# The second gate one expert earlier, and low parts of weights on VectorE while it is worked out

## The chip, the cores and the metric

One core of one Trainium2 chip. The metric is device time in microseconds of one execution; the kernel before has a median of 983.49 us in 3 runs (981.95 to 984.66). TensorE multiplies matrices; VectorE, ScalarE and GpSimd work on tiles in SBUF (GpSimd also issues the indirect DMAs); SyncE (SP) issues the other DMAs. Each engine takes its instructions in the order in which the kernel writes them.

## The reference

Causal block attention (4 batches, 8 heads, 576 positions of 64), then two layers of experts over 2304 tokens of width 512. In the first, each token goes to its best two of eight experts, in the second to one. Cut to the routing and one expert:

```
noisy = x @ w_gate + log1p(exp(x @ w_noise)) * noise
top2  = two largest of noisy, weighted by their softmax
for e in range(8):                      # first layer, 512 -> 1024 -> 512
    out[mask] += top2_w * (relu(x[mask] @ w1[e]) @ w2[e])
logits = out @ w_gate2 + modality_bias[modality_id]
e_idx  = argmax(logits)                 # second layer: one expert each
out2[mask] = softmax(logits)[e_idx] * (relu(out[mask] @ m2w1[e]) @ m2w2[e])
```

## The kernel before

Each matrix is split into a high part, which TensorE takes in a fast format (`wh`, `xth`, `hh`), and a low part, the rest (`wl`, `xtl`, `hl`); a product is three matmuls. ScalarE casts the high part; the low part is a subtraction. For weights that subtraction (`Stage.split`, 128 x 1024) is on the engine that the caller hands in.

The work after attention is a list of jobs that `run` (line 1418) goes through. A job is one expert (or part of one) over a group of tokens: its first half, `mm1`, makes eight blocks of the hidden layer; its second, `mm2`, makes one tile of 128 tokens at a time in PSUM (three such tiles, `py`). During `mm1`, `run` splits this job's second weights and gathers the next job's token rows (`rows`, an indirect DMA on GpSimd); during `mm2` it transposes the rows that have been gathered (`cols`: TensorE into the one tile `px`, ScalarE `xth`, VectorE `xtl`) and splits the next job's first weights (`between`).

Order of the jobs: parts of experts 0 and 1, the rest of 0, experts 2 to 7 (five token tiles each; E is 8, so E-3, E-2 and E-1 are experts 5, 6 and 7), and then the second layer's six groups (`seconds`): groups 1 and 2 of 512 tokens from the first table (k = 0), groups 3 and 4 of 512 and two of 256 from the second (k = 1). The expert of a group is known only at run time and is read into a register on SP.

When a tile of a first-layer expert is done, its rows are added to `X2` in DRAM by an indirect DMA, and eight dot products on VectorE (`zero<-py,gts,wide`, reading the result in PSUM) give what it adds to the second gate's logits; a further indirect DMA adds them to `LG`, with a 1 that counts how many of its two experts a token has behind it. After the last such add of a job, its `then` is called.

`gates(k)` (line 1478) is a generator of some eighty small steps, nearly all on VectorE. It loads `LG` (`lgx`), takes the tokens that are complete (k = 0) or complete and not yet placed (k = 1), counts them by expert (small matmuls into `pt`), fixes which expert each group gets (`eg0`, `eg1`, `egs`) and writes lists of slots (`ids00`, `ids10`, `ids11`: `sl_ob`, `sl_oa`, `sl_ov`, matmuls into `pt`, then `si_*`). `starts` gives counts and first groups per expert, `experts_of` the expert of each group. For k = 1 it also makes `more` and `eo`, which only a loop at the very end of the kernel reads.

The order of instructions on every engine is written out by a planner: `clk` adds up a modelled cost of each instruction, `walk` runs a generator's steps at modelled times, `filler` puts waiting dot products in whenever VectorE's modelled clock is at most 0.4 us (0.2 while the flag `chain` is set, that is while `gates` runs) ahead of TensorE's, and `room` forces out the oldest ones when more than two tiles of them wait. A job's gathers are issued once the flag of its slots is set.

Of the kernel before, what the change touches and what calls it, by code (L numbers as in the profile page):

```python
# [30 lines left out]
def moe_kernel(tc, q, k, v, w_gate, w_noise, noise, w1, w2, mod_id, w_gate2, mod_bias, m2w1, m2w2, out):  # L31
# [25 lines left out]
    def bc(ap, shape):  # L57
        return ap.to_broadcast(shape)
# [47 lines left out]
    with ExitStack() as top:  # L106
# [362 lines left out]
        class Job:  # L469
# [21 lines left out]
            def gather(s, t):  # L491
                xr = rp.tile([128, DM], F32, name="xr", bufs=5)
                i = gps.indirect_dma_start(out=xr, out_offset=None, in_=s.table,
                                                 in_offset=bass.IndirectOffsetOnAxis(ap=s.ic(t), axis=0))
                if s.apart is not None:
                    for o in s.apart:
                        tc.declare_no_dep(i.ins, o.ins, reason="rows of other tokens")
                    early_rows.append(i)
                s.xr.append(xr)
                if s is j11:  # L500
                    s.due.append(max(clk["dve"], clk["pool"]) + 2.5)
# [96 lines left out]
        last_rows, early_rows = [], []  # L598

        def add_rows(ids, c0, nt, then=None):  # L600
            last = c0 + nt == NA1
            prev = last_rows if last else []
            placed_ = []

            def f(t, yr, py, g):
                c = c0 + t
                i = gps.indirect_dma_start(out=X2, out_offset=bass.IndirectOffsetOnAxis(ap=ids[:, c:c + 1], axis=0),
                                                 in_=yr, in_offset=None, compute_op=OP.add)
                for o in prev + (early_rows if last else []):
                    tc.declare_no_dep(i.ins, o.ins, reason="rows of other tokens")  # L610
                prev.append(i)
                note(yr, py, g, ids[:, c:c + 1], placed_, then if t == nt - 1 else None)
            return f

        def job1(e, t0=0, nt=NP, then=None, need=(None, None)):
            return Job((w1[e], w2[e]), X1, nt, lambda t: ids1[:, e * NP + t0 + t:e * NP + t0 + t + 1],
                       lambda t: gts1[:, e * NP + t0 + t:e * NP + t0 + t + 1], add_rows(ids1, e * NP + t0, nt, then), need, 128 if nt == 2 else UNIT)
# [35 lines left out]
        j11.wa, j11.wb = j10.wa, j10.wb  # L653
        chain = lambda k, p: lambda: walk(gates(k), now[0] + .5, p)
        firsts = [job1(0, FIRST[0], NP - FIRST[0], need=(None, "ids1"))]
        firsts += [job1(e, then={E - 2: chain(0, 1), E - 1: chain(1, 1)}.get(e), need=(None, "ids1")) for e in range(2, E)]
        seconds = [job2(k, g) for k in range(2) for g in range(NW)] + [job2(1, g, True) for g in range(NSM)]
        stage = Stage([j00, j10] + firsts + seconds)

# [758 lines left out]
        def run(jobs, hp_, ea, eb, nxt=None, stage=stage):  # L1418

            ah = 4  # L1420
            fs = (0, 1, 3, 5)
            for n, j in enumerate(jobs):
                nx = jobs[n + 1] if n + 1 < len(jobs) else nxt

                def rows():
                    if nx and nx.ready(1) and len(nx.xr) < nx.nt:
                        nx.gather(len(nx.xr))

                eb_ = [gps, gps, vec, vec] if j is firsts[0] else eb
                for f in range(len(j.hh), NF // 128):  # L1430
                    j.mm1(f, hp_)
                    if f in fs and len(j.wb) < NQ:
                        stage.split(eb_[fs.index(f) % len(eb_)] if "ids1" in flags else vec)
                    stage.fetch(ah)
                    rows()
                    filler()
                    tick(j.n * .005)
                left = [0, 0, 2 * j.nt]

                def between():  # L1440
                    left[2] -= 1
                    if nx:
                        if left[2] == 0 and not nx.ready(1):
                            until(nx.need[1])
                        while left[2] < 2 and nx.ready(1) and len(nx.xr) < nx.nt:
                            nx.gather(len(nx.xr))
                        while left[0] < len(nx.xr) and (left[2] == 0 or left[0] < 2 * j.nt - left[2]):
                            if left[2] and left[0] < len(nx.due) and nx.due[left[0]] > clk["pe"]:
                                break
                            nx.cols(left[0])  # L1450
                            left[0] += 1
                            if nx is j10 and left[0] == nx.nt:
                                at(clk["pe"] + .5, spread)
                            if left[2] >= nx.nt - left[0]:
                                break
                        while len(nx.wa) < NQ and left[1] < NQ * (2 * j.nt - left[2]) / (2 * j.nt):
                            if not stage.ring and not nx.ready():
                                if left[2]:
                                    break
                                until(nx.need[0])  # L1460
                            stage.split(ea[left[1] % len(ea)] if "ids1" in flags else vec)
                            left[1] += 1
                    stage.fetch(ah)
                    filler()
                    tick(2.56)

                for t in range(j.nt):
                    j.mm2(t, between)
                    rows()
                    between()  # L1470
# [7 lines left out]
        def gates(k):  # L1478
# [37 lines left out]
            if k == 1:  # L1516
                nr = pool.tile([128, E], F32, name="g_nr")
                vec.scalar_tensor_tensor(nr, gn, -float(GW), pp[:, NTT], op0=OP.mult, op1=OP.add)
                yield .3
                gm, gr = yield from starts(pool, nr, th2, "q_")  # L1520
                yield from experts_of(pool, gm, gr, egs, "q_")
                flags.add("egs")
                vec.tensor_scalar(gr, gr, 2.0, float(BW * NW), op0=OP.mult, op1=OP.add)
                yield .3
                vec.scalar_tensor_tensor(gr, gn, -float(BW), gr, op0=OP.mult, op1=OP.add)
                yield .3
                vec.tensor_add(nr, gs, gn)
                yield .3
                vec.tensor_scalar(nr, nr, NW + .5, 1e5, op0=OP.is_gt, op1=OP.mult)
                yield .3  # L1530
                vec.tensor_add(gs, gs, nr)
                yield .3
                go, s_ = yield from starts(pool, base, th1, "o_")
                vec.tensor_copy(gso, s_)
                yield .3
                yield from experts_of(pool, go, gso, eo, "o_")
            t0, pos, st = tl("t0", sh), tl("pos"), tl("st")
            vec.tensor_tensor(t0, pp[:, 0:NTT], oh, op=OP.mult)
            yield .3
# [14 lines left out]
                vec.scalar_tensor_tensor(w, s2, float(GW), pos, op0=OP.mult, op1=OP.is_gt)  # L1554
                yield .3
            if k == 1:
                vec.tensor_tensor(t0, oh, bc(gr[:, None, :], sh), op=OP.mult)
                yield .3
                vec.tensor_reduce(s2, t0, axis=AX, op=OP.add)
                yield .3  # L1560
                vec.scalar_tensor_tensor(st, st, float(BW), s2, op0=OP.mult, op1=OP.subtract)
                yield .3
                vec.tensor_tensor(st, st, w, op=OP.mult)
                yield .3
                vec.tensor_add(st, st, s2)
                yield .3
# [7 lines left out]
            if k < 2:  # L1574
                new = tl("new") if k else placed
                vec.tensor_scalar(new, a, cap - .5, None, op0=OP.is_lt)
                yield .3
                if k:
                    vec.tensor_add(placed, placed, new)
                    yield .3  # L1580
                    held = tl("held", dt=BF16)
                    vec.tensor_copy(held, placed)
                    yield "pe", 0
                    pm = ps_r.tile([128, NTT], F32, name="pt")
                    ten.matmul(pm, ones, held, start=True, stop=True)
                    yield .4
                    m = pool.tile([1, 1], F32, name="g_m")
                    vec.tensor_reduce(m, pm[0:1], axis=AX, op=OP.add)
                    yield .3
                    vec.tensor_scalar(more, m, float(NT) - .5, None, op0=OP.is_lt)  # L1590
                    yield .3

            vec.tensor_tensor(l, l, bc(mx[:, :, None], sh), op=OP.subtract)
# [11 lines left out]
            for i0_, a0 in enumerate(range(0, cap, 2 * HG)):  # L1605
# [9 lines left out]
                yield .3  # L1615
                yield from slot_ids(pool, acc, na, NTT, pad2[:, a0:a0 + na], ids[:, a0:a0 + na], gts[:, a0:a0 + na])
                flags.add("ids%d%d" % (k, i0_ > 0))
            flags.discard("chain")

        with sp():  # L1620
# [131 lines left out]
```

## Time and profile before

| | |
|---|---|
| median of 3 runs | 983.49 us |
| profiled execution | 984.59 us, its span 982.8 us, mean granted clock 0.989 |
| VectorE busy | 681.4 us (69%) |
| ScalarE busy | 482.6 us (49%) |
| GpSimd busy | 489.6 us (50%) |
| HBM | 126 GB/s over the span |

Busy is the sum of the times in which an engine ran something; the idle time of an engine that sets no end costs nothing. Stages follow each other in time: attention until about 300 us, the first layer until 738, the second to the end.

### The profile page before, as it was taken

To read this page: it belongs to the slowest core of one execution; us is meant where nothing else is said; L and a number is where in the kernel's file an instruction comes from. 1 tells how busy PE (TensorE), PEld (TensorE's weight loads), DVE (VectorE), ACT (ScalarE), POOL (GpSimd) and SP (SyncE) were. 2 spreads that over 40 slices of the span, in tenths; PEclk is the share of its full clock that TensorE was granted. 3 is DMA by queue.
4 is the path that set the end of the run, shared out by engine and by line. 5 is a ranking of instruction groups with operands and counts; after the bars stand their busy time and mean duration, and the time that the engine had idled before them with its cause. 6 is when DMAs were issued, how large, how long until landed. Compare 5 with 4: busy or idle time off the path is not lost.

```text
span 982.8 us, 16351 instructions
## 1 busy us (share of the span) xinstructions
PE 943.6 (96%) x5661; PEld 835.6 (85%) x5661; DVE 681.4 (69%) x1676; ACT 482.6 (49%) x1090; POOL 489.6 (50%) x472
## 2 busy tenths in 40 slices
PE   9999998999999999999999999999889988999995
PEld 6989897998978999989898998989767876888894
DVE  6878779888889979395775939577877764433241
ACT  6989997987651344333333333433223332433352
POOL 6234343464325599585875848557374124222122
PEclk9999999999999999999999999999999999999998
DMA  6586742322196366374654627443554525443440
GB/s 128 104 216 192 233 122 70 78 60 68 58 337 156 68 187 165 111 158 97 130 128 116 122 76 171 99 76 47 161 113 124 181 79 175 137 130 108 138 130 13
DMA packets 145293, 124.49 MB, mean 127 GB/s; under 512 B 75626, under 2 KB 115946, under 8 KB 145075
## 3 DMA queue, kind: packets, MB, share of 16 engines
q1 hardware_dynamic: 126242, 90.14, 32.0%
q0 software_dynamic: 17904, 32.96, 16.7%
q8 instruction: 47, 0.77, 0.3%
q10 hardware_dynamic: 1056, 0.26, 0.1%
q14 instruction: 44, 0.35, 0.1%
HBM read 95.50 MB, written 28.09 MB: 126 GB/s over the span
## 4 chain that ended last, share of the span: by engine, by line
PE 70%; issue 11%; DVE 6%; POOL 5%; ACT 4%; DMA 3%; SPq 0%; POOLq 0%; ACTq 0%; DVEq 0%
PE py L73 25%; PE ph L73 25%; PE pt L73 8%; PE ps L73 6%; PE pa L73 3%; POOL wl L73 2%; PE px L73 2%; ACT p L73 2%; DMA raw<-in_moe_w_dram 1%; DVE wl L73 1%; DMA xr<-X,ids 1%; DVE PTl L73 1%; ACT kp L73 1%; DMA qld<-in_q_dram 1%; POOL out_dram L73 1%
## 5 line engine op out<-in xcount | busy, mean ns | idle before, releaser
L73 POOL TENSOR_TENSOR wl<-raw,wh 128x1024 fp32r<-128x1024 f32 x70 | 180.9, 2602 | 113.8 <-ACT wh L73 111.2
L73 DVE SCALAR_TENSOR_TENSOR zero<-py,gts,wide 128x512 f32<-128x512 f32 x304 | 227.6, 749 | 8.4
L73 PE MATMUL ph<-xth,wh 128*128 128x312 f32 (+4 forms) x672 | 217.2, 323 | 2.1 <-DVE kp L73 1.2
L73 PE MATMUL ph<-xtl,wh 128*128 128x312 f32 (+4 forms) x672 | 216.9, 323 | 0.2 <-DVE xtl L73 0.2
L73 PE MATMUL ph<-xth,wl 128*128 128x312 f32 (+4 forms) x672 | 217.1, 323 | 0.0
L73 PE MATMUL py<-wh,kp 128*128 128x512 f32 x488 | 166.0, 400 | 0.0
L73 PEld LDWEIGHTS ph<-xth,wh 128*128 128x128 f32 x672 | 127.4, 190 | 8.5 <-DVE kp L73 1.9
L73 PEld LDWEIGHTS ph<-xtl,wh 128*128 128x128 f32 x672 | 127.3, 189 | 6.0 <-DVE xtl L73 0.5
L73 PEld LDWEIGHTS ph<-xth,wl 128*128 128x128 f32 x672 | 126.9, 189 | 5.2
L73 ACT ACTIVATE yr<-py,gts 128x512 f32<-128x512 f32 x59 | 40.6, 688 | 165.0 <-PE py L73 109.3
L73 ACT ACTIVATE wh<-raw 128x1024 fp32r<-128x1024 f32 x112 | 117.8, 1052 | 2.1 <-DMA raw<-in_moe_w_dram 2.1
L73 PEld LDWEIGHTS py<-wh,kp 128*128 128x128 f32 x488 | 92.4, 189 | 19.0
L73 DVE SCALAR_TENSOR_TENSOR hl<-ph,hh 128x312 fp32r<-128x312 f32 (+5 forms) x84 | 43.0, 514 | 78.8 <-ACT hh L73 78.7
L73 PE MATMUL ps<-kh,kp 128*128 128x256 f32 (+5 forms) x320 | 95.9, 340 | 0.5 <-ACT p L73 0.3
L73 PE MATMUL py<-wl,kp 128*128 128x512 f32 x244 | 96.0, 394 | 0.0
L73 PE MATMUL py<-wh,hh 128*128 128x512 f32 x228 | 94.3, 413 | 0.0
L73 POOL DMA_INDIRECT xr<-X,ids x54 | 56.1, 1040 | 76.2 <-PE px L73 43.3
L73 PE MATMUL py<-wh,hl 128*128 128x512 f32 x228 | 90.9, 399 | 0.0
L73 PE MATMUL py<-wl,hh 128*128 128x512 f32 x228 | 90.5, 397 | 0.0
L73 ACT ACTIVATE hh<-ph 128x312 fp32r<-128x312 f32 (+5 forms) x84 | 38.4, 457 | 99.8 <-PE ph L73 99.6
L73 DVE TENSOR_TENSOR xtl<-px,xth 128x512 fp32r<-128x512 f32 (+1 forms) x57 | 38.9, 682 | 64.6 <-ACT xth L73 64.6
L73 ACT ACTIVATE kp<-ph 128x312 fp32r<-128x312 f32 (+5 forms) x84 | 38.4, 457 | 91.8 <-PE ph L73 91.4
(274 smaller groups left out, 1843.0 us busy)
## 6 DMA issues: line engine op xcount, KB each, us to landing
raw<-in_moe_w_dram SPq DMA_DIRECT2D x112, 512.0 KB, 3.6
X<-zero SPq DMA_DIRECT2D x13, 512.0 KB, 4.0
kld<-in_k_dram SPq DMA_DIRECT2D x32, 128.0 KB, 2.9
vld<-in_v_dram SPq DMA_DIRECT2D x32, 128.0 KB, 2.8
X<-x SPq DMA_DIRECT2D x16, 256.0 KB, 2.7
qld<-in_q_dram SPq DMA_DIRECT2D x30, 128.0 KB, 3.0
wide<-in_moe_w_dram SPq DMA_DIRECT2D x4, 512.0 KB, 5.7
wide<-WG2T POOLq DMA_DIRECT2D x1, 2048.0 KB, 10.2
```

Source lines behind the costliest of these rows:

```text
L73: return f(*a, **kw)
```

## The change

`gates(0)` is started by the last logits of expert E-3 instead of E-2, so it takes the tokens that are complete behind experts 0 to 5; the first two groups' gathers are declared free of the row additions of both last experts. While the flag `chain` is set, `Stage.split` gets VectorE whatever the caller's choice. In `gates(1)`, the experts of the small groups come behind the first list of slots, and the parts that only the loop at the end needs come last; a tile `g_gb` takes what was written over `gr`.

```diff
@@ gather
-                    for o in s.apart:
+                    for o in sum(s.apart, []):
@@ add_rows
-            last = c0 + nt == NA1
-            prev = last_rows if last else []
-            placed_ = []
+            late = c0 >= (E - 2) * NP
+            prev, placed_ = [], []
+            if late:
+                last_rows.append(prev)
...
-                for o in prev + (early_rows if last else []):
+                for o in prev + (early_rows if late else []):
@@ the jobs
-        firsts += [job1(e, then={E - 2: chain(0, 1), E - 1: chain(1, 1)}.get(e), need=(None, "ids1")) for e in range(2, E)]
+        firsts += [job1(e, then={E - 3: chain(0, 1), E - 1: chain(1, 1)}.get(e), need=(None, "ids1")) for e in range(2, E)]
@@ run
-                        stage.split(eb_[fs.index(f) % len(eb_)] if "ids1" in flags else vec)
+                        stage.split(eb_[fs.index(f) % len(eb_)] if "ids1" in flags and "chain" not in flags else vec)
...
-                            stage.split(ea[left[1] % len(ea)] if "ids1" in flags else vec)
+                            stage.split(ea[left[1] % len(ea)] if "ids1" in flags and "chain" not in flags else vec)
@@ gates, k == 1
                 gm, gr = yield from starts(pool, nr, th2, "q_")
-                yield from experts_of(pool, gm, gr, egs, "q_")
-                flags.add("egs")
-                vec.tensor_scalar(gr, gr, 2.0, float(BW * NW), op0=OP.mult, op1=OP.add)
+                gb = pool.tile([128, E], F32, name="g_gb")
+                vec.tensor_scalar(gb, gr, 2.0, float(BW * NW), op0=OP.mult, op1=OP.add)
...
-                go, s_ = yield from starts(pool, base, th1, "o_")
-                vec.tensor_copy(gso, s_)
-                yield .3
-                yield from experts_of(pool, go, gso, eo, "o_")
...
-                    held = tl("held", dt=BF16)
-                    vec.tensor_copy(held, placed)
-                    yield "pe", 0
-                    pm = ps_r.tile([128, NTT], F32, name="pt")
-                    ten.matmul(pm, ones, held, start=True, stop=True)
...
                 flags.add("ids%d%d" % (k, i0_ > 0))
+                if k == 1 and i0_ == 0:
+                    yield from experts_of(pool, gm, gr, egs, "q_")
+                    flags.add("egs")
+            if k == 1:
+                go, s_ = yield from starts(pool, base, th1, "o_")
...
+                yield from experts_of(pool, go, gso, eo, "o_")
+                held = tl("held", dt=BF16)
+                vec.tensor_copy(held, placed)
+                yield "pe", 0
+                pm = ps_r.tile([128, NTT], F32, name="pt")
+                ten.matmul(pm, ones, held, start=True, stop=True)
...
             flags.discard("chain")
```

## Rows read from the trace of the kernel before

**Rows 1.** The page, busy time, share of the span and instructions of TensorE.

```profile
PE 943.6 (96%) x5661; PEld 835.6 (85%) x5661; DVE 681.4 (69%) x1676; ACT 482.6 (49%) x1090; POOL 489.6 (50%) x472
```

**Rows 2.** Five stages, busy PE PEld DVE ACT POOL, then clock, DMA, GB/s.

```profile
610.50:668.20 57.70, 57.70 (x334) 52.20 (x334) 39.72 (x102) 20.64 (x34) 35.57 (x19) 1.00 0.48 99
668.20:737.90 69.70, 63.00 (x367) 54.57 (x365) 54.81 (x147) 21.34 (x35) 41.72 (x26) 0.95 0.45 105
737.90:785.20 47.30, 46.86 (x228) 38.45 (x229) 36.66 (x96) 16.61 (x23) 15.72 (x11) 1.00 0.52 150
785.20:841.90 56.70, 51.39 (x247) 40.07 (x246) 31.61 (x73) 17.61 (x25) 19.32 (x15) 0.94 0.43 130
841.90:887.30 45.40, 45.40 (x210) 37.56 (x209) 15.79 (x19) 17.30 (x24) 10.67 (x8) 1.00 0.44 138
```

**Rows 3.** TensorE's waits, 600 to 983 us: in total, times, longest.

```profile
PE px L73 <- DMA xr<-X,ids: 4.5, 3, 2.8
PE pt L73 <- DVE sl_ov L73: 2.7, 1, 2.7
PE pt L73 <- DVE g_held L73: 2.5, 1, 2.5
PE px L73 <- DVE xtl L73: 1.4, 1, 1.4
PE ph L73 <- ACT xth L73: 0.9, 1, 0.9
```

**Rows 4.** The same columns for the first and last stretch of low clock.

```profile
708.60:711.90 3.30, 3.30 (x16) 2.40 (x16) 3.16 (x9) 0.00 (x0) 0.00 (x0) 0.50 0.53 159
...
821.30:824.50 3.20, 3.20 (x10) 2.62 (x9) 1.85 (x4) 1.54 (x2) 2.50 (x3) 0.50 0.71 223
```

**Rows 5.** Instructions in order of time (start, duration): VectorE's, and one of GpSimd.

```profile
700.63 2.38 DVE L73 TENSOR_TENSOR vals<-g_t,vals 128x18 bf16<-128x18 f32 x1
...
704.41 4.02 DVE L73 TENSOR_TENSOR sl_ov<-sl_oa,vals 128x360 bf16<-128x360 bf16 x1
...
705.13 2.90 POOL L73 TENSOR_TENSOR wl<-raw,wh 128x1024 fp32r<-128x1024 f32 x1
...
714.28 0.53 DVE L73 TENSOR_TENSOR sl_ov<-sl_oa,vals 128x360 bf16<-128x360 bf16 x1
...
792.50 2.32 DVE L73 TENSOR_TENSOR sl_a<-sl_a,g_msk 128x18 f32<-128x18 f32 x1
```

**Rows 6.** VectorE alone: two stretches, three groups (628.9 to 668.3), one low part.

```profile
686.50:720.40 33.90, 30.32 (x83) 0.95 0.47 125
628.90:668.30 39.40, 25.46 (x64) 1.00 0.46 93
...
L73 DVE SCALAR_TENSOR_TENSOR zero<-py,gts,wide 128x512 f32<-128x512 f32 x26 | 19.5, 750 | 0.9
L73 DVE SCALAR_TENSOR_TENSOR hl<-ph,hh 128x312 fp32r<-128x312 f32 x7 | 3.4, 482 | 8.7 <-ACT hh L73 8.7
L73 DVE TENSOR_TENSOR xtl<-px,xth 128x496 fp32r<-128x496 f32 (+1 forms) x5 | 3.4, 675 | 5.6 <-ACT xth L73 5.6
...
765.20 1.23 DVE L73 TENSOR_TENSOR wl<-raw,wh 128x1024 fp32r<-128x1024 f32 x1 [0.26 <-ACT wh L73]
```

**Rows 7.** Start and duration: TensorE in E-2, logits added, SP's queue, first gather.

```profile
654.42 13.92 PE py L73 x60
...
681.32 1.56 POOL L73 DMA_INDIRECT LG<-yg,ids  x1 [1.48 <-DVE zero L73]
...
684.44 0.34 SPq L1489 DMA_DIRECT2D lgx<-LG  x1
695.71 53.51 SPq L451 DMA_DIRECT2D raw<-in_moe_w_dram  x12
...
764.32 1.56 POOL L73 DMA_INDIRECT LG<-yg,ids  x1 [5.21 <-DVE zero L73]
...
816.43 2.14 POOL L73 DMA_INDIRECT xr<-X,ids  x1 [6.26 <-DVE si_g L73]
```

More of the change, by code (lines that the diff above doesn't have):

```diff
@@ L1520, in gates @@
                 gm, gr = yield from starts(pool, nr, th2, "q_")
-                yield from experts_of(pool, gm, gr, egs, "q_")
-                flags.add("egs")
-                vec.tensor_scalar(gr, gr, 2.0, float(BW * NW), op0=OP.mult, op1=OP.add)
+                gb = pool.tile([128, E], F32, name="g_gb")
+                vec.tensor_scalar(gb, gr, 2.0, float(BW * NW), op0=OP.mult, op1=OP.add)
                 yield .3
-                vec.scalar_tensor_tensor(gr, gn, -float(BW), gr, op0=OP.mult, op1=OP.add)
+                vec.scalar_tensor_tensor(gb, gn, -float(BW), gb, op0=OP.mult, op1=OP.add)
                 yield .3
@@ L1556, in gates @@
             if k == 1:
-                vec.tensor_tensor(t0, oh, bc(gr[:, None, :], sh), op=OP.mult)
+                vec.tensor_tensor(t0, oh, bc(gb[:, None, :], sh), op=OP.mult)
                 yield .3
@@ L1579, in gates @@
                     vec.tensor_add(placed, placed, new)
-                    yield .3
-                    held = tl("held", dt=BF16)
-                    vec.tensor_copy(held, placed)
-                    yield "pe", 0
-                    pm = ps_r.tile([128, NTT], F32, name="pt")
-                    ten.matmul(pm, ones, held, start=True, stop=True)
[L1586 to L1590, printed above, removed]
                     yield .3
@@ L1617, in gates @@
                 flags.add("ids%d%d" % (k, i0_ > 0))
+                if k == 1 and i0_ == 0:
[3 more added lines that the diff above has]
+                go, s_ = yield from starts(pool, base, th1, "o_")
+                vec.tensor_copy(gso, s_)
+                yield .3
+                yield from experts_of(pool, go, gso, eo, "o_")
[4 more added lines that the diff above has]
+                ten.matmul(pm, ones, held, start=True, stop=True)
+                yield .4
+                m = pool.tile([1, 1], F32, name="g_m")
+                vec.tensor_reduce(m, pm[0:1], axis=AX, op=OP.add)
+                yield .3
+                vec.tensor_scalar(more, m, float(NT) - .5, None, op0=OP.is_lt)
+                yield .3
             flags.discard("chain")
```

## Prediction

> **What bounds the kernel now.** I read the page's busy shares first: TensorE is busy 943.6 us of a span of 982.8 [rows 1], so only what TensorE waits for, and the stretches in which its clock is low, can be won. Second, the table of stages. The second-last expert (E-2) takes 57.7 us with TensorE never idle at clock 1.00; the last (E-1) takes 69.7 at 0.95; group 1 takes 47.3, group 2 takes 56.7 at 0.94, and group 3, the same matmuls as group 2 with no gates beside them, 45.4 [rows 2]. So E-1 and group 2 hold nearly all that can go. Third, the waits of TensorE from 600 us on: five rows, 4.5 + 2.7 + 2.5 + 1.4 + 0.9 = 12.0 us: for the gathered rows `xr`, twice for `gates` (`sl_ov`, `g_held`), for `xtl`, for `xth` [rows 3]. Fourth, the clock: four stretches of at least 3.2 us behind these waits run at 0.50, that is at 1.2 GHz instead of 2.4 GHz; the first and the last are shown [rows 4]. Each loses half of 3.3 us, some 1.65, four lose 6.6; the stages agree, 5% of 69.7 and 6% of 56.7 being 6.9 [rows 2]. Everything that the change can win is 12.0 + 6.6 = 18.6 us.
>
> **Why TensorE waits there.** `gates(0)` begins when the last logits of E-2 are added (681.32) and `lgx` is loaded (684.44), 16 us into E-1 [rows 7], and holds VectorE from 686.5 to 720.4 [rows 6]. Group 1's gathers need its slots, so they come at the very end of E-1, where its transposes want them: 1.7 us of the 4.5 us (the longest, 2.8, is group 2's), the 1.4 and the 0.9 [rows 3]. The 2.7 us wait is VectorE's lateness: `sl_ov` took 4.02 us at 704.41 and 0.53 at 714.28; the long one ends when GpSimd's `wl` (705.13, 2.90 us) does. `vals` took 2.38 us at 700.63 beside a `wl`, where steps of that size take 0.2, and `sl_a` 2.32 at 792.50 [rows 5]. So GpSimd's low parts hold VectorE up by about 3.5 + 2.2 + 0.3 = 6.0 us in `gates(0)` and 2.1 in `gates(1)` (the 0.3 is a smaller one, an estimate). The `sl_a` is what `g_held` and its 2.5 us wait come from.
>
> The Trainium skill, "SBUF — State Buffer", section "Who interferes with whom", says that a VectorE instruction with two SBUF inputs and a GpSimd instruction that reads SBUF exclude each other, the later one waiting for the whole of the earlier. The trace agrees (4.02 us against 0.53). Without that rule 4.02 could be the operation's own cost and would move with it; VectorE would then be 6.0 us later in E-2 and the time about 975.5 us.
>
> **Part 1: gates(0) during E-2.** Moved are: on SP one `lgx` load and the register load of the groups' experts; on VectorE all of `gates(0)`; one Exp on ScalarE; about 1.6 us of small matmuls (E-1's surplus over E-2 is 12.0; its waits 6.9 less a few tenths and its lost clock 3.5 leave that). All shift by one stage, 57.7 us: `lgx` to about 626.7, VectorE's first step to 628.8. SP queues E-1's weight loads behind that `lgx`. Before, SP stood from before 684.44 to its next weight load at 695.71 [rows 7], with no wait of TensorE for weights in the list [rows 3]; up to four tiles of weights are loaded ahead. I cost this at 0; uncovered it would be the 3 us that lie between the logits' add and `lgx`. GpSimd gets no new work: the four gathers of group 1 go from the end of E-1 into its first matmul half, where GpSimd has no gathers now, and the earlier gathers free their buffers during E-2. So E-1 becomes a stage like E-2, and the waits 1.7 + 1.4 + 0.9 go, with one half-clock stretch.
>
> What is late next is VectorE in E-2. Today it works 25.46 of the 39.4 us from 628.9 to 668.3, idle because nothing is due [rows 6]. The dot products with the second gate's weights (0.79 us each: 750 ns and a read-out behind it) read the result straight from PSUM, with three PSUM tiles: TensorE can't begin the fifth token tile before the second one's dots are through, 16 dots in all. What VectorE must do from 628.8 until then:
> - `gates(0)`: 33.9 us of window less 13 dots (10.3), seven `hl` at about 0.4 net (2.8) and 6.0 held up = 14.8, its own short waits included;
> - six `hl` of 0.48: 2.9; five `xtl` of 0.68: 3.4;
> - three low parts that the new flag moves to VectorE, 1.23 + 0.26 waiting for ScalarE's high part: 4.5;
> - 16 dots: 12.6.
>
> The sum is 38.2, so they are through at 667.0. TensorE would begin the fifth tile at 654.42 + 13.92 x 36/60 = 662.8 [rows 7], with the small matmuls 1.6 at 664.4. VectorE is 2.6 us late: this wait takes the place of the 2.7 for `sl_ov`. Its bounds are 0 (if dots fit into the pauses in which `gates` waits for TensorE or ScalarE) and 7 (if VectorE waits in turn for small matmuls queued behind the waiting result, and a fourth split falls under the flag). I take 2.6 and add one half-clock stretch, 1.65, since each of the longest waits of before has one behind it. Queued behind the waiting matmul on TensorE are the rest of E-2 and all of E-1; nothing else is in a hurry then. The single transpose tile is a second, smaller place: the `xtl` of one transposition must be through before the next, about 3.2 us later, and now stands among gate steps. I put it at 0.3 (0 to 2).
>
> **Part 2: low parts on VectorE while the flag is set.** GpSimd's split went beside these steps; on VectorE each costs 1.5 us of a queue that is in order. In E-2 that is 4.5 us (counted above) for 6.0 taken off. In group 2's first half two splits change hands, 3.0 for 2.1. So VectorE is about even, and what is won is that no single step is held for 2 to 3.5 us.
>
> **Part 3: the order inside gates(1).** Sixteen VectorE steps (0.14 to 0.3 us each, about 3.5 together) go behind the first list of slots. Also, `gates(1)` starts earlier. E-1's last logits now come at 764.32, 26.4 us after the stage's end at 737.9; E-2's came 13.1 after its own (681.32 against 668.2) [rows 2, 7]. With nothing but dots left in E-1 it becomes 13.1 again. From that add to group 2's first gather it is 52.1 us now (816.43), and 52.1 - 2.1 - 3.5 + 3.0 = 49.5 then: 62.6 us after group 1 begins. Group 2's first half ends at about 47 + 23 = 70. So the gathers go out in the first half, and the 2.8 us wait goes with its half-clock stretch; so does the 2.5 for `g_held`, whose matmul stands at the end. For small waits for list steps with more on VectorE I leave 0.2 (0 to 2).
>
> **Sum.** -12.0 - 6.6 + 2.6 + 1.65 + 0.3 + 0.2 = -13.85 us. The profiled execution took 984.59 (span 982.8 and 1.8 around it), which gives 970.7; it lies 1.1 above the median of the three runs, 983.49, on which the same sum gives **969.7 us**.
>
> **The rivals.**
> - *VectorE keeps up in E-2.* For it: it is idle there for 13.9 us, and the planner puts dots into pauses. Against: the demand above. All 18.6 go but some tenths: 965.
> - *Group 2's gathers are still late.* The order is written out by a planner with its own costs; if the slots come in the second half, the transpose stands right behind its gather and 2.8 + 1.65 stay, with perhaps another of the size of 2.5: 974 to 977. Against it stand 7 us of margin (62.6 against 70). It decides if `gates(1)` is more than 7 us longer than worked out.
> - *The groups can't be filled.* With one expert less, fewer tokens are complete, and what doesn't fit goes to a loop at the end. Running the reference's routing on its inputs, 1188 tokens are complete behind six experts, 588 and 600 of the only two second-layer experts in use; 512 of each are wanted, so the same two groups come out full. If not, at least one group's 45.4 us would be added: 1015. Chance 1 in 100.
> - *Slower: VectorE's queue in E-2 stops TensorE at every transpose.* Place: the five transposes and two PSUM tiles of E-2's second half. An `xtl` behind some gate steps and a low part (1.5) would come 2 to 3 us late. If all five do, with the fourth and fifth tile 7 us late and TensorE at half clock for most of 30 us, that is 12 + 7 + 13 = 32, less 18.6: 997. It decides once the queue ahead of each `xtl` exceeds the 2 us that the transposes leave. Against it: in group 1's second half gate steps, low parts and `xtl` stand together today, and the list of waits has only 1.4 us for `xtl` in all [rows 3].
>
> **How the numbers follow.** About 0.3% (3 us) can be told from no change here. Forecast, 966.5 to 973.5: 0.50. VectorE keeps up, 964 to 966.5: 0.22. Late gathers or more waits in E-2, 973.5 to 980: 0.17. Within 3 us of before: 0.05. Slower, by either of the last two rivals: 0.06. So faster 0.89, same 0.05, slower 0.06. The range 964.5 to 977.5 leaves out a little of the second case, the upper part of the third, and the last two.
>
> **What would show it.** E-1 in 58 to 59 us at clock 1.00; no TensorE wait for `xr` from 600 us on; `lgx` at about 627 and again 13 us into group 1; no `sl_ov` over 0.6 us; group 2 in 47 to 48 us; and in E-2 a TensorE wait at `py` for `zero` (the dots) of 2 to 4 us, the only new one. I am wrong if E-2 has no such wait (time near 965), if it is over 8 us, or if the wait for `xr` is still there.

## The result, and the profile after

The changed kernel takes 971.76 us (969.18 to 972.32, 4 runs) against 982.72 for the kernel before (980.44 to 984.66, 4 runs): a ratio of 0.9875, 95% interval 0.985 to 0.990, or 11 us less. The profiled execution took 972.32 us, its span 970.5 (984.59 and 982.8 before).

The table of stages after: E-2, E-1, groups 1, 2 and 3; busy PE, PEld, DVE, ACT, POOL with counts, then clock, DMA share, GB/s. It answers to [rows 2].

```profile
612.60:677.90 65.30, 61.75 (x372) 54.39 (x371) 55.36 (x153) 20.98 (x35) 29.31 (x19) 0.97 0.49 111
677.90:735.10 57.20, 57.20 (x330) 51.77 (x329) 41.22 (x106) 20.11 (x33) 38.09 (x22) 1.00 0.52 110
735.10:781.80 46.70, 46.50 (x229) 38.38 (x228) 35.71 (x99) 17.64 (x25) 14.14 (x9) 1.00 0.47 139
781.80:829.90 48.10, 47.79 (x247) 37.84 (x246) 30.63 (x67) 17.29 (x24) 13.53 (x13) 1.00 0.53 166
829.90:875.30 45.40, 45.40 (x209) 37.56 (x209) 15.66 (x18) 17.30 (x24) 10.67 (x8) 1.00 0.40 129
```

E-1 fell from 69.7 us to 57.2 and group 2 from 56.7 to 48.1; E-2 rose from 57.7 to 65.3, with 3.5 us of TensorE idle and clock 0.97. The four stages from E-2 to group 2 take 217.3 us where they took 231.4: 14.1 less. The profile's span fell by only 12.3, because E-2 begins at 612.6 instead of 610.5, in work that the change does not touch; another execution of the same kernel begins it at 609.4 (e5 below).

TensorE's waits after, from 600 us on (in total, times, longest), against [rows 3]:

```profile
PE py L73 <- DVE zero L73: 3.6, 2, 3.2
PE pt L73 <- issue: 0.3, 1, 0.3
PE pt L73 <- DVE g_oh L73: 0.2, 1, 0.2
```

Every wait of [rows 3] is gone; the new one, for the dot products, is the one that part 1 of the prediction worked out. Of the four half-clock stretches [rows 4] one is left, right behind that wait (columns as in the table of stages):

```profile
671.20:674.50 3.30, 3.30 (x10) 2.56 (x9) 3.12 (x11) 0.00 (x0) 3.00 (x3) 0.50 0.75 192
```

VectorE in front of the long wait (start, duration, in brackets the idle time before and what ended it):

```profile
661.38 0.16 DVE L73 TENSOR_TENSOR si_g<-g_acc 128x8 f32<-128x8 f32 x1
662.86 1.23 DVE L73 TENSOR_TENSOR wl<-raw,wh 128x1024 fp32r<-128x1024 f32 x1 [1.31 <-ACT wh L73]
664.00 0.21 DVE L73 TENSOR_TENSOR gts<-si_g,g_acc 128x8 f32<-128x8 f32 x1
664.13 0.74 DVE L73 SCALAR_TENSOR_TENSOR zero<-py,gts,wide 128x512 f32<-128x512 f32 x1
```

A low part that stands in VectorE's order ahead of the second tile's dots waits 1.31 us for ScalarE's high part and takes 1.23: 2.5 us in which no dot runs, while TensorE is about to need them. The high part was late because it stood in ScalarE's order right behind a read-out, `yr`, that had waited 2.60 us for TensorE's third tile:

```profile
661.19 0.69 ACT L73 ACTIVATE yr<-py,gts 128x512 f32<-128x512 f32 x1 [2.60 <-PE py L73]
661.77 1.05 ACT L73 ACTIVATE wh<-raw 128x1024 fp32r<-128x1024 f32 x1
```

GpSimd and SP after, against [rows 7]: the gathers for group 1, the last logits of E-1, the first gather from the second table, and the two loads of `lgx`.

```profile
665.86 1.02 POOL L73 DMA_INDIRECT xr<-X,ids  x1 [0.31 <-issue]
...
755.71 1.56 POOL L73 DMA_INDIRECT LG<-yg,ids  x1 [0.17 <-DVE hl L73]
...
798.54 1.07 POOL L73 DMA_INDIRECT xr<-X,ids  x1 [14.75 <-DVE si_g L73]
```

```profile
628.79 0.34 SPq L1490 DMA_DIRECT2D lgx<-LG  x1
...
758.61 0.34 SPq L1490 DMA_DIRECT2D lgx<-LG  x1
```

The first `lgx` comes 16.2 us into E-2, where the prediction put it. The second comes 23.5 us into group 1, where the prediction's list of signs has 13 (its sum gives 16: the last add at 13.1 and the 3.1 us from add to load). The first gather of the second table (rows for group 3, fetched during group 2, which the prediction calls group 2's first gather) nevertheless comes at 63.4, where 62.6 was worked out: two errors that cancel (below).

### The profile page after: what moved, and what is told of

It is laid out like the page before. It is cut to its first block, busy times and chain, and to the rows that moved or that the text cites. A ratio compares the mean times of both kernels' runs of the same rounds, so it can differ in the third digit from the quotient of the medians.

```text
span 970.5 us, 16357 instructions
## 1 busy us (share of the span) xinstructions
PE 938.6 (97%) x5661; PEld 832.7 (86%) x5661; DVE 683.2 (70%) x1683; ACT 483.2 (50%) x1090; POOL 472.3 (49%) x465
## 4 chain that ended last, share of the span: by engine, by line
PE 79%; DVE 9%; ACT 5%; issue 4%; DMA 1%; POOL 1%; POOLq 0%; ACTq 0%; DVEq 0%
PE ph L73 30%; PE py L73 29%; PE pt L73 8%; PE ps L73 6%; PE pa L73 4%; PE px L73 2%; ACT p L73 2%; DVE wl L73 1%; DVE zero L73 1%; DVE PTl L73 1%; ACT kp L73 1%; DVE nm L73 1%; DVE sl_ob L73 1%; ACT wh L73 1%; DMA raw<-in_moe_w_dram 1%
## 5 line engine op out<-in xcount | busy, mean ns | idle before, releaser
L73 POOL TENSOR_TENSOR wl<-raw,wh 128x1024 fp32r<-128x1024 f32 x63 | 164.2, 2626 | 77.4 <-ACT wh L73 69.8
L73 POOL DMA_INDIRECT X<-yr,ids x40 | 64.7, 1617 | 53.3 <-ACT yr L73 43.9
L73 DVE TENSOR_TENSOR wl<-raw,wh 128x1024 fp32r<-128x1024 f32 x49 | 63.4, 1295 | 33.7 <-ACT wh L73 33.6
```

The source lines that it names most:

```text
L73: return f(*a, **kw)
```

## The experiments

Theory: three things cost time, each cured by a part of its own: `gates(0)` beginning too late (part 1), steps held up by GpSimd's low parts (part 2), the slots of `gates(1)` coming too late (part 3), and VectorE's total work in E-2 then sets the new wait. Rivals: GpSimd's low parts are the main cause; or the order of steps, not the sum of work, makes the new wait.

Lengths of the stages in the profiles (from the first matmul of a stage's first half to that of the next):

| kernel | E-2 | E-1 | group 1 | group 2 | sum | median us | ratio to before, 95% |
|---|---|---|---|---|---|---|---|
| before | 57.6 | 69.7 | 47.3 | 56.6 | 231.3 | 982.72 | |
| part 1 alone (e1) | 61.9 | 57.2 | 46.7 | 51.2 | 217.0 | 969.12 | 0.9851 (0.9829 to 0.9872) |
| part 2 alone (e2) | 57.6 | 69.9 | 46.9 | 53.4 | 227.9 | 981.05 | 0.9983 (0.9972 to 0.9994) |
| part 3 alone (e3) | 57.6 | 68.6 | 47.4 | 49.5 | 223.2 | 974.95 | 0.9921 (0.9892 to 0.9951) |
| parts 1 and 3 (e4) | 61.8 | 57.2 | 46.7 | 48.1 | 213.9 | 966.46 | 0.9826 (0.9805 to 0.9846) |
| changed, again (e5) | 65.2 | 57.2 | 46.6 | 48.1 | 217.1 | 969.20 | 0.9869 (0.9838 to 0.9901) |
| one split back (e6) | 61.1 | 57.2 | 46.7 | 48.1 | 213.1 | 965.85 | 0.9831 (0.9800 to 0.9861) |
| half the dots (e7) | 59.5 | 57.2 | 46.7 | 48.0 | 211.5 | 964.25 | 0.9814 (0.9784 to 0.9845) |
| lists later (e8) | 58.5 | 58.2 | 46.6 | 48.2 | 211.5 | 964.25 | 0.9816 (0.9790 to 0.9842) |
| parts 1 and 2 (e9) | 65.0 | 57.2 | 46.7 | 48.1 | 217.1 | 971.10 | 0.9885 (0.9847 to 0.9922) |
| e8, part 2 in gates(1) (e10) | 58.5 | 58.2 | 46.7 | 48.1 | 211.4 | 964.21 | 0.9815 (0.9776 to 0.9854) |

Each ratio is to the kernel before as run beside it: 982.75 us for e1 to e4, 980.72 for e5 to e8 (another chip), 982.64 for e9 and e10 (a third). The stages show more than the medians do, since E-2 begins between 609.4 and 612.6 us in these profiles.

**e1, part 1 alone.**

```diff
-        firsts += [job1(e, then={E - 2: chain(0, 1), ...
+        firsts += [job1(e, then={E - 3: chain(0, 1), ...
...
+            late = c0 >= (E - 2) * NP
```

> Only the earlier start of gates(0), with its two lists of row additions; low parts stay on GpSimd and gates(1) keeps its order. Theory (the start decides): E-1's waits of 1.7 + 1.4 + 0.9 us and its half-clock stretches go, and gates(1) starts 13 us earlier, so group 2's 2.8 us goes too. Left are steps held up by GpSimd's low parts: in E-2 6.0 us of holding up in place of 4 x 1.5 us of low parts on VectorE, so a wait of some 3.5 us at `py` or at a list matmul as in the changed kernel, and one of about 2.5 us for `g_held` or a list in gates(1): about 975 (973 to 978). Rival (GpSimd's low parts decide): E-2 shows 6 us or more of waits and the time is 979 or above.

Measured: 13.6 us less than before, at least all that the whole change gives. E-1 is repaired as expected. The wait in E-2 is smaller than I said; its waits, and group 2's one of 2.0:

```profile
PE pt L73 <- DVE sl_ov L73: 2.6, 2, 2.0
PE py L73 <- DVE zero L73: 0.9, 1, 0.9
PE px L73 <- DVE xtl L73: 0.4, 1, 0.4
PE pt L73 <- DVE g_oh L73: 0.2, 1, 0.2
```

The 975 was a miss, by what happens in E-2: I had taken over the 6.0 us of holding up from E-1 and expected a wait of 3.5 us, and its waits are 0.7, 0.9 and 0.4 with no half-clock stretch behind them. In E-2 GpSimd's low parts meet other steps; in order of time, both engines of this kernel:

```profile
643.83 2.40 POOL L73 TENSOR_TENSOR wl<-raw,wh 128x1024 fp32r<-128x1024 f32 x1 [8.75 <-ACT wh L73]
643.87 2.43 DVE L73 TENSOR_TENSOR vals<-g_t,vals 128x18 bf16<-128x18 f32 x1
646.19 1.35 DVE L73 TENSOR_TENSOR sl_ob<-lane,sl_b 128x1152 bf16<-128x1152 f32 x1
...
651.15 2.38 POOL L73 TENSOR_TENSOR wl<-raw,wh 128x1024 fp32r<-128x1024 f32 x1 [2.18 <-ACT wh L73]
652.13 2.61 DVE L73 TENSOR_TENSOR sl_ob<-lane,sl_b 128x1152 bf16<-128x1152 f32 x1
```

`vals` is held for 2.2 us (0.22 elsewhere), the second `sl_ob` for 1.3 (1.35 at 646.19), one earlier step for 0.3: 3.8 us, not 6.0. A low part beside the dots, at 664.01, held none of them up.

**e2, part 2 alone.**

```diff
-                        stage.split(eb_[fs.index(f) % len(eb_)] if "ids1" in flags else vec)
+                        stage.split(eb_[fs.index(f) % len(eb_)] if "ids1" in flags and "chain" not in flags else vec)
```

> Only the low parts on VectorE while the flag is set; gates(0) still starts after E-2. Theory (the start decides): the 2.7 us for `sl_ov` and the 2.5 for `g_held` go with about two half-clock stretches, but group 1's gathers still come at E-1's end (waits for `xr`, `xtl`, `xth` of 3 to 4 us stay) and group 2's 2.8 us stays: a gain of 4 to 7 us, 976 to 979. Rival (GpSimd's low parts decide): a gain of 9 us or more, 974 or below.

Measured: a gain of 1.7 us, less than the theory (4 to 7) or the rival (9) had it. The waits for `sl_ov` and `g_held` did go (0.5 is left), but others grew:

```profile
PE px L73 <- DMA xr<-X,ids: 5.7, 2, 3.2
PE py L73 <- DVE zero L73: 2.9, 1, 2.9
PE ph L73 <- ACT xth L73: 1.7, 2, 0.9
PE px L73 <- DVE xtl L73: 1.4, 1, 1.4
```

Taking the low parts from GpSimd cures the held-up steps and, with `gates(0)` still in E-1, brings the wait for the dots there. The rival that the low parts are the main cause falls.

**e3, part 3 alone.**

```diff
-                yield from experts_of(pool, gm, gr, egs, "q_")
...
+                if k == 1 and i0_ == 0:
+                    yield from experts_of(pool, gm, gr, egs, "q_")
```

> Only the order inside gates(1): the experts of the small groups, the parts for the loop at the end and the `g_held` matmul go behind the lists. Theory: the 2.5 us for `g_held` goes with its half-clock stretch, unless the held-up `sl_a` then delays a list matmul; the slots come 3 to 5 us earlier, still in group 2's second half, so a wait for `xr` of 0 to 2.8 us stays: a gain of 2 to 6 us, 977 to 981, all of it in group 2. Rival (order is without weight): within 2 us of before.

Measured: 7.8 us, more than expected, nearly all in group 2 (56.6 to 49.5). The wait for `xr` there is 0.3 instead of 2.8, `g_held` is gone, one wait of 1.3 for `sl_ov` remains, and there is no half-clock stretch in group 2. Of the 7.1 us there, the waits make 3.7 and the two half-clock stretches that are gone 3.4. TensorE's longest waits from 600 us on; all but the 1.3 and 0.3 are E-1's:

```profile
PE pt L73 <- DVE sl_ov L73: 4.0, 2, 2.8
PE px L73 <- DMA xr<-X,ids: 2.1, 2, 1.8
PE px L73 <- issue: 1.7, 2, 1.4
```

**e4, parts 1 and 3: the change with low parts left on GpSimd.** The two lines of e2 undone.

> The change without its second part: low parts stay on GpSimd while the flag is set. Theory (VectorE is about even, what it gains is that no step is held 2 to 3.5 us): E-2's waits are 3 to 6 us against the changed kernel's 3.5, gates(1) shows one wait of up to 2 us: 971 to 976, that is 0 to 4 us above the changed kernel. Rival (GpSimd's low parts decide): 5 us or more above it, 977 or higher, with a `sl_ov` of 2 us or longer in front of the longest wait. A third way: below the changed kernel, if the four low parts on VectorE cost the dot products more than the holding up does.

The third way came: 966.46 us, and 213.9 in the four stages against 217.2 with part 2. All of the difference is E-2, 61.8 against 65.2; one profile more without part 2 has 61.9 there (e1), two more with it 65.2 and 65.0 (e5, e9).

```profile
PE pt L73 <- DVE sl_ov L73: 1.1, 2, 0.7
PE py L73 <- DVE zero L73: 0.9, 1, 0.9
PE px L73 <- DVE xtl L73: 0.4, 1, 0.4
PE pt L73 <- DVE g_oh L73: 0.2, 1, 0.2
```

In the changed kernel four low parts between the start of `gates(0)` and the fifth tile put 4.9 us and about 1.7 of waiting for ScalarE on VectorE (five are moved in all, one of them before the first step of `gates(0)`); leaving them on GpSimd costs the 3.8 us of e1. Three of the four in the changed kernel; the fourth, at 662.86, is shown above:

```profile
634.91 1.23 DVE L73 TENSOR_TENSOR wl<-raw,wh 128x1024 fp32r<-128x1024 f32 x1 [0.15 <-ACT wh L73]
...
646.06 1.23 DVE L73 TENSOR_TENSOR wl<-raw,wh 128x1024 fp32r<-128x1024 f32 x1 [0.27 <-ACT wh L73]
...
653.02 1.22 DVE L73 TENSOR_TENSOR wl<-raw,wh 128x1024 fp32r<-128x1024 f32 x1
```

**e5, the changed kernel again**, beside the next three.

> The changed kernel as it is, beside the next three on one chip: 970 to 973.

Measured: 969.20, just below; E-2 again 65.2 with waits of 3.2 and 0.4.

**e6, one low part of E-2 back on GpSimd.**

```diff
-                            stage.split(ea[left[1] % len(ea)] if "ids1" in flags and "chain" not in flags else vec)
+                            stage.split(gps if nx is firsts[-1] and left[1] == 2 else
+                                        ea[left[1] % len(ea)] if "ids1" in flags and "chain" not in flags else vec)
```

> The changed kernel, but the third low part of E-2's second half goes back to GpSimd; on VectorE it took 1.23 us and 1.31 of waiting for ScalarE's high part, right in front of the dots that TensorE waits for. Theory (the wait at `py` is VectorE's work added up, low parts included): the wait of 3.2 us shrinks by 2.4 to 0.8, its half-clock stretch goes too: 3 to 5 us below the changed kernel, 966.5 to 969. Rival (the wait comes from the order in which gate steps go ahead of the dots, not from the low parts): the wait stays above 2 us and the time within 1.5 us of the changed kernel.

```profile
PE py L73 <- DVE zero L73: 1.1, 2, 0.7
PE pt L73 <- issue: 0.3, 1, 0.3
PE pt L73 <- DVE g_oh L73: 0.2, 1, 0.2
```

As the theory said: the long wait fell by 2.5 us, from 3.2 to 0.7, and its half-clock stretch went; E-2 is 4.1 us shorter. The median, 965.85, is 3.4 below e5, inside the 3 to 5 that I gave, though 0.7 below the times that I gave with it.

**e7, half the dots in E-2** (it leaves out four of eight second-gate logits of E-2's tokens).

```diff
-            fill.extend([(t, lambda e=e: dot(e), direct) for e in range(E)])
+            fill.extend([(t, lambda e=e: dot(e), 2 * direct if half else direct)
+                         for e in ((1, 2, 4, E - 1) if half else range(E))])
```

> The changed kernel, but E-2's token tiles make only four of the eight dot products (the logits of second-layer experts 0, 3, 5 and 6 miss what E-2 adds). Theory (VectorE's throughput in E-2 sets the wait): 16 dots become 8 before the fifth tile, 6.3 us less, so both waits at `py` are gone and with them the half-clock stretch: E-2's stage is 5 us shorter and the time 4.5 to 6 us below the changed kernel. Rival (a gate step or a semaphore holds TensorE, not the sum): a wait of 1 us or more is left in E-2.

```profile
PE pt L73 <- issue: 0.3, 1, 0.3
PE pt L73 <- DVE g_oh L73: 0.2, 1, 0.2
```

The median is 964.25. Both waits at `py` are gone and E-2 is 5.7 us shorter (59.5). With e6 this settles the new wait: VectorE's work up to the fifth tile sets it, whether a low part (with its wait for ScalarE) or half the dots are taken away.

**e8, the lists of `gates(0)` later, low parts on GpSimd.**

```diff
+                if k == 0:
+                    yield 28
                 pl = ps_r.tile([128, NV, na], F32, name="pt")
```

> The changed kernel with low parts left on GpSimd, and in gates(0) the two lists of slots put off by 28 us of the planner's time, into E-1's first half. Theory (gates(0) has tens of us to spare once it starts in E-2, so its lists should not stand before the dots): E-2's waits of 0.7 + 0.4 + 0.9 us go, gathers for group 1 still come before its transposes: 963.5 to 965.5, 1 to 3 us below the kernel without the second part (966.5). Rival (the slots are then late again): a wait for `xr` of 1 us or more at E-1's end, time 967 or above.

```profile
PE pt L73 <- DVE sl_ov L73: 0.5, 1, 0.5
PE pt L73 <- DVE g_oh L73: 0.2, 1, 0.2
```

As the theory said: 964.25, E-2 (58.5) and E-1 (58.2) both at clock 1.00 without a wait, the two in the list being those of groups 1 and 2, and the gathers (from 687.55) still well before their transposes at 699.6. It beats both kernels, 0.9816 of before.

**e9, the change without its third part.** The lines of e3 undone.

> The change without its third part: gates(0) early, low parts on VectorE, gates(1) in its old order. Theory (the third part matters only where a held-up step or late slots stand in gates(1), and neither is there any more): E-2 has its 3.5 us of waits as in the changed kernel, group 2 has no wait over 1 us, the time is within 1.5 us of the changed kernel beside it (969 to 972 by earlier runs). Rival (the third part is worth by itself what it was worth alone, 7.8 us): 975 or above, with a wait for `xr` or `g_held` in group 2.

```profile
PE py L73 <- DVE zero L73: 3.5, 2, 3.2
PE pt L73 <- DVE sl_ov L73: 0.5, 1, 0.5
PE pt L73 <- DVE g_oh L73: 0.2, 1, 0.2
```

The changed kernel was not run beside it, but each has its kernel before: the time is 11.5 us under that, as for the changed kernel in e5. The profile has 0.5 us of wait for `sl_ov` in group 2 and nothing for `xr` or `g_held`. With parts 1 and 2 in place, part 3 gains nothing in the sum (217.1 against 217.1). From the last logits of E-1 to the first gather it takes 49.1 us (754.43 to 803.57) against 42.8 in the changed kernel, a head start that nothing uses.

**e10, e8 with low parts on VectorE in `gates(1)` only.** A flag set for k = 1 takes the place of `chain` in the two lines of e2.

> The kernel with the lists of gates(0) put off and low parts on GpSimd, but on VectorE while gates(1) runs. Theory (a held-up step in gates(1) is all that is left): the 0.5 us wait for `sl_ov` goes, nothing else changes: 963 to 964.5, equal to the kernel with the lists put off within 1 us. Rival (low parts on VectorE cost in gates(1) what they cost in E-2): 2 us or more above it.

964.21: nothing gained, nothing lost; a wait of 0.3 for `g_held` stands where 0.5 for `sl_ov` was.

## Why the prediction was right, point by point

- *What can be won* (18.6 us): right, and a little low. E-1 and group 2 lost all the waits of [rows 3] and their half-clock stretches. e8 takes 19.8 us out of the four stages (231.3 to 211.5); 0.7 of it is group 1 (47.3 to 46.6), which the 18.6 leave out.
- *Part 1.* E-1 became a stage like any other (57.2 us at 1.00; e1 shows that part 1 does this alone). The new wait at `py` is where it was put. The cost of 0 for SP's queue held: no wait of TensorE for weights came up. VectorE was to be through at 667.0; allowing for the 2.0 us by which E-2 begins later, 669.0, and TensorE went on at 670.5. The term that was mis-sized is the low parts: four, not three, lie in that stretch, the fourth with 1.31 us of waiting, 2.5 us together; the rest of the sum came out about 1 us too high. TensorE came to that tile at 667.3, 0.9 later than worked out (666.4 with the later start). The wait is 3.2 + 0.3 instead of 2.6, and the one half-clock stretch is there.
- *Where the gathers go.* I had group 1's gathers in E-1's first half. They are issued from 665.86 on, in E-2's second half, soon after the slots are there (`gts` at 664.00). The planner writes them in E-1's first half, so GpSimd does not run in the order in which the kernel writes, as I had said of every engine; the kernel fixes the order (`manual_schedule`) of TensorE, ScalarE and VectorE there, not of GpSimd. It cost nothing.
- *Part 2, "VectorE is about even": wrong.* The 6.0 us of holding up belonged to E-1's order of steps. In E-2 it is 3.8 (e1), against some 6.6 for the low parts. With its half-clock stretch part 2 costs 3.3 us in the sum (e4 against the changed kernel). It pays where `gates(1)` has a held-up step and nothing else removes it (part 2 alone on group 2: 56.6 to 53.4; on top of part 1, e1 to e9: 51.2 to 48.1).
- *Part 3.* The gathers of the second table do come in group 2's first half. But `gates(1)` began 7.6 us later than I had it: E-1's last logits are added 20.7 us into group 1 (755.71), not 13.1. Group 1's first half takes the dots more slowly than an expert's does; why was not tried. And `gates(1)` took 42.8 us from there, not 49.5: 9.3 less than before. With part 1 alone (e1) it takes 52.2; the new order takes 9.0 off that (e4, from 750.15 to 793.38: 43.2), part 2 takes 3.1 (e9, 49.1), both together 9.4: what one has taken the other can hardly take again. The prediction had 3.5 for the order and part 2 costing 0.9. I had counted the sixteen steps' busy time and not the planner's pauses between them; that these are the rest was not tried. Nor did the two waits need part 3: the 2.8 for `xr` is gone with part 1 alone (e1), and neither that nor the one for `g_held` is there in e9, which has the old order.
- *The sum.* -13.85 was forecast, and the four stages give -14.1. That it fits so closely is luck in part. By the prediction's terms E-2 would take 63.9 us (57.7 + 1.6 + 2.6 + 1.65 + 0.3) and takes 65.3; E-1, group 1 and group 2 came out shorter than their terms by about as much together. The medians give -11.0. Of the 3 us between, 2.1 are E-2's later start in the profile after; the profiled execution before is also 1.9 above its median, the one after 0.6. Where the executions without a profile differ is not on record. The kernel before ran at mean clocks from 0.989 to 0.993 beside e1, so the number of half-clock stretches may be a part of it. (983.49 less 13.85 is 969.6, not 969.7, and the 975.5 for VectorE 6.0 later would be 975.6; nothing hangs on either.)
- *The rival with full gain* was not what this change does, but it could be had: e8 comes to 964.25, by moving the lists behind the dots and leaving the low parts on GpSimd.

The parts don't add: 14.3, 3.4 and 8.1 us alone in the sum of stages make 25.8, together 14.1. Part 1 alone gives what all three give; parts 1 and 3 give 17.4, and part 2 takes 3.3 back.

## What to carry to other kernels

When a block of work moves to another stage, count again in that stage both what it will be held up by and what its new neighbours ask of the same engine up to the next point where TensorE needs a result; neither moves along unchanged. Relieving an idle helper engine by the one whose queue sets the next wait can cost more than the collisions that it avoids. Of a chain that has become early, the late half can be put off again behind work that is due.

## What the runs showed of the hardware that was not expected

- Not every long wait has a half-clock stretch behind it. In e3 TensorE waited 2.77 us for `sl_ov` in E-1 and went on at 707.84 at clock 1.00; in e1 a wait of 1.98 us, ending at 789.19, had low clock behind it; the changed kernel's 3.2 had one in each of two profiles. In e2 one low stretch of about twice the length (0.55 from 722.9 to 726.2, 0.50 from 726.6 to 730.0) followed a wait of 3.16 and held another of 2.87. So the 1.65 us that the prediction adds for each long wait is what most of them cost here, not a rule. The stretches behind the waits of e3 and e1 (columns as in the table of stages; in e1 the fall comes inside the stretch):

```profile
707.80:711.20 3.40, 3.36 (x22) 2.64 (x23) 3.26 (x9) 0.59 (x1) 0.00 (x0) 1.00 0.57 154
```

```profile
789.20:792.40 3.20, 3.20 (x18) 2.45 (x19) 2.94 (x3) 0.00 (x0) 0.00 (x0) 0.73 0.26 49
```

- A cast with one input in SBUF was held up as well: in e1 `vals<-g_t` (128 x 18, to bf16) took 2.15 us at 784.32 beside GpSimd's `wl` from 784.02 to 786.41, where it takes 0.20 alone. The dots, which read PSUM, are not: 0.75 us beside a `wl` in e1's E-2. The Trainium skill, "SBUF — State Buffer", section "Who interferes with whom", counts casts among the operations that can take the pair of ports shared with GpSimd; the trace agrees.

```profile
784.02 2.39 POOL L73 TENSOR_TENSOR wl<-raw,wh 128x1024 fp32r<-128x1024 f32 x1 [5.87 <-ACT wh L73]
...
784.32 2.15 DVE L73 CAST vals<-g_t 128x18 bf16<-128x18 f32 x1
```
